# Tail of an attention and feed-forward kernel: which engine makes the remainders, and when the token blocks are renewed

## The chip, the cores and the metric

The kernel runs on one core of one Trainium2 chip. The metric is the device time of one launch, in microseconds (us). The kernel before takes 994.36 us (median of 3 runs, 994.13 to 994.58). The execution that the hardware profiler recorded took 986.7 us, of which 984.7 us are the span of instructions that the views below show.

## The reference

Attention with a forgetting factor over 4 batches, 8 heads, 576 positions and 64 dimensions is followed by two feed-forward parts on the 2304 tokens of width 512:

```python
scores = scale * np.matmul(q, k.transpose(0, 1, 3, 2)) + decay      # causal, softmax
x = np.matmul(attn, v)                                              # 2304 x 512
h = x @ w_in                                                        # 512 -> 2048
g = h * np.tanh(np.log1p(np.exp(h)))                                # mish
y = g @ w_out                                                       # 2048 -> 512
a, b = y @ w1, y @ w2                                               # 512 -> 1024 each
out = ((a * b) @ w3) @ w_out2                                       # 1024 -> 1024 -> 512
```

All of it is float32, and w3 and w_out2 are multiplied with each other ahead of use, so behind the attention there are three layers: the first one (w_in and mish), the K layer "g" (w_out), the M layer "g" (w1 and w2 and their product), and the K layer "h" (w3 times w_out2). They run for two halves of the tokens, q = 0 and q = 1.

## The kernel before, in words

**Float32 from faster products.** Every operand of a product is held as two fp32r parts: hi, a copy rounded by ScalarE, and lo, the remainder x - hi, a subtraction. TensorE makes hi*hi, hi*lo and lo*hi (`MM_PAIRS`). So each block that TensorE reads costs one ScalarE cast and one subtraction. `halves` (lines 927 to 930) writes both; the subtraction of every second block is made by VectorE and the others by GpSimd (`k % 2`).

**Seven products for eight.** Every layer multiplies 2 x 2 blocks in seven products, numbered 1 to 7, with sums and differences of blocks as operands. In a K layer (`k_layer`, n = 8 rows of blocks for g and 4 for h) the products run in `ORDER_K` = 1, 2, 6, 5, 7, 3, 4, and for each product over n tiles. One tile is twelve matmuls of 288 columns on TensorE. Its operand is made by `operand` (lines 909 to 925) from the four blocks b11, b12, b21, b22 of the source, which are renewed in place with sums (128 x 576 subtractions on VectorE): before, two of them stand behind product 2's operand (b11 and b12) and two in product 6 (its own operand raw, and b21). `k_begin` makes operands `T_AHEAD` = 4 tiles ahead; all of them live in a ring of 12 buffers (`x_tile`), two for a tile and three for a tile of product 6. Where such a layer ends, `m_operands` (line 1003 on) makes the 14 operands of the M layer from its four result blocks.

In an M layer (`m_layer`, line 1026 on) one step m is seven products of twelve matmuls; ScalarE copies some banks and VectorE adds the others (lines 1051, 1053, 1055). Products 1, 6, 7 and 4 of one m write the same bank, and between 7 and 4 only product 1 of the next m runs, so the add behind product 7 (line 1055) has that long.

**Other work in the tail.** In the first layer `s_sums` and `s_build` (lines 1091 and 1108) make weight operands for step m + 1 (sp0 and sp1, the remainder on GpSimd at line 1113), and the M layer of q = 0 builds its weights in `gate_sums` and `gate_build` (remainder on GpSimd at line 892). `x_operands` (line 1060) makes the first layer's operands while TensorE works off the last units of line 554, whose results VectorE copies out (h, line 559).

**What sets the order.** TensorE runs in written order. The other engines are placed by a scheduler that works with a simulated timeline; each of them then runs strictly in its own order, and an instruction that waits holds up all behind it on that engine. `between` makes the scheduler place instructions behind the last marked one of each engine.

Of the kernel before, what the change touches and what calls it, by code (L numbers as in the profile page):

```python
# [14 lines left out]
ALU = mybir.AluOpType  # L15
# [51 lines left out]
def f32(ap):  # L67
    return ap.bitcast(F32)
# [8 lines left out]
class Kernel:  # L77
# [807 lines left out]
    def gate_build(self, m, x, ps):  # L885

        n = len(ps)
        w = self.w_ring(f"gs{m}_{ps[0]}")
        v = w[:, :512 * n].rearrange("p (n h w) -> p n h w", n=n, h=2)
        x = x.rearrange("p (n w) -> p n w", n=n)  # L890
        self.nc.scalar.copy(v[:, :, 0], x)
        self.nc.gpsimd.tensor_tensor(v[:, :, 1], x, f32(v[:, :, 0]), ALU.subtract)
        for i, o in enumerate(ps):
            self.gate[m, o] = w[:, 512 * i:512 * i + 512]
            self.nc.sync.dma_start(self.ws[1][self.place(1, m, o)], f32(self.gate[m, o]))
# [10 lines left out]
        a, b = [t.rearrange("p (r h w) -> p r h w", r=2, h=2) for t in (src[f], src.get(f + n, src[f]))]  # L906
        return a[:, :, 0], a[:, :, 1], b[:, :, 0], b[:, :, 1]

    def operand(self, name, o, b, k):

        b11, b12, b21, b22 = b
        tt = self.nc.vector.tensor_tensor
        hi, lo = [self.x_tile(f"{name}_{x}").rearrange("p (r w) -> p r w", r=2) for x in "hl"]
        raw = {1: b11, 2: b21, 3: b22, 4: b21, 5: b11, 7: b12}.get(o)
        if o == 6:
            raw = self.x_tile(f"{name}_r", F32).rearrange("p (r w) -> p r w", r=2)
            tt(raw, b22, b11, ALU.subtract)
            self.halves(raw, hi, lo, k)
            tt(b21, b21, raw, ALU.subtract)
            return hi, lo  # L920
        self.halves(raw, hi, lo, k)
        if o == 2:
            tt(b11, b12, b11, ALU.subtract)  # L923
            tt(b12, b22, b12, ALU.subtract)
        return hi, lo

    def halves(self, raw, hi, lo, k):
        self.mark(self.nc.scalar.copy(hi, raw))  # L928
        eng = self.nc.vector if k % 2 else self.nc.gpsimd
        self.mark(eng.tensor_tensor(lo, raw, f32(hi), ALU.subtract))  # L930

    def mark(self, ins):

# [9 lines left out]
    def k_begin(self, name, n, src):  # L943

        seq = [(o, f) for o in ORDER_K for f in range(n)]
        ops = {}

        def ready(i):
            if i < len(seq) and i not in ops:
                o, f = seq[i]  # L950
                ops[i] = self.operand(f"{name}{o}_{f}", o, self.quarters(src, f, n), i)

        for i in range(T_AHEAD):
            ready(i)
        return n, seq, ops, ready
# [47 lines left out]
    def m_operands(self, q, c, T, raw, os):  # L1003

        add = self.nc.vector.tensor_tensor
        for o in os:
            for k in range(2):
                b11, b12, b21, b22 = [c[k][:, i] for i in range(4)]
                if o in (5, 6, 7, 4):
                    raw[o, k] = self.x_tile(f"r{q}_{o}_{k}", F32).rearrange("p (r w) -> p r w", r=2)  # L1010
                else:
                    raw[o, k] = {1: b11, 2: b21, 3: b22}[o]
                x = raw[o, k]
                if o == 5:
                    add(x, b12, b11, ALU.subtract)
                elif o == 6:
                    add(x, b22, raw[5, k], ALU.subtract)
                elif o == 7:
                    add(x, b22, b12, ALU.subtract)
                elif o == 4:  # L1020
                    add(x, b21, raw[6, k], ALU.subtract)
                t = self.big(0, f"T{q}_{o}_{k}", F32R) if o in (2, 4) else self.t_tile(f"T{q}_{o}_{k}")
                T[o, k] = t.rearrange("p (h r w) -> p h r w", h=2, r=2)
                self.halves(x, T[o, k][:, 0], T[o, k][:, 1], len(T))

    def m_layer(self, name, T, get, post, hook):

# [32 lines left out]
    def x_operands(self, T, os):  # L1060

        tt = self.nc.vector.tensor_tensor
        n = 0
        for o in os:
            for k in range(2):
                b11, b12, b21, b22 = [[self.xr[8 + 4 * r + c][:, TB * h:TB * h + TB] for r in range(2)]
                                      for c in (k, k + 2) for h in range(2)]
                tmp = self.tmp[:, k]
                t = self.w_ring(f"TX{o}_{k}") if o in (7, 4) else self.t_tile(f"TX{o}_{k}")
                t = T[o, k] = t.rearrange("p (h r w) -> p h r w", h=2, r=2)  # L1070
                if o == 5:
                    for r in range(2):
                        tt(tmp[:, r], b12[r], b11[r], ALU.subtract)
                elif o == 6:
                    for r in range(2):
                        tt(tmp[:, r], b22[r], tmp[:, r], ALU.subtract)
                elif o == 4:
                    for r in range(2):
                        tt(tmp[:, r], b21[r], tmp[:, r], ALU.subtract)
                elif o == 7:  # L1080
                    for r in range(2):
                        tt(b12[r], b22[r], b12[r], ALU.subtract)
                if o in (5, 6, 4):
                    self.halves(tmp, t[:, 0], t[:, 1], n)
                    n += 1
                    continue
                for r in range(2):
                    self.halves({1: b11, 2: b21, 3: b22, 7: b12}[o][r], t[:, 0, r], t[:, 1, r], n)
                    n += 1

    def s_sums(self, m):

# [15 lines left out]
    def s_build(self, m, i):  # L1108

        v = self.sp[m % 2][i].rearrange("p (n h w) -> p n h w", n=2, h=2)  # L1110
        x = self.vs[m][i].rearrange("p (n w) -> p n w", n=2)
        self.nc.scalar.copy(v[:, :, 0], x)  # L1112
        self.nc.gpsimd.tensor_tensor(v[:, :, 1], x, f32(v[:, :, 0]), ALU.subtract)  # L1113

    def first_layer(self, cover):

# [190 lines left out]
```

## Time and profile before

| | us |
|---|---|
| median of 3 runs | 994.36 |
| the profiled execution | 986.7 |
| its span | 984.7 |
| TensorE busy in the span | 891.0 |
| VectorE busy | 666.5 |
| ScalarE busy | 496.9 |
| GpSimd busy | 447.1 |

The attention part ends at about 371 us of the span. Busy time of VectorE and GpSimd in the views includes time in which an instruction has started and cannot go on, so the same instruction is long in one place and short in another; a mean over all of them hides that. "Idle before" at a row names the instruction that ended the wait.

### The profile page before, as it was taken

The page shows a single profiled execution, that of the slowest core. Times are in us where ns is not written, and L with a number is a line of the kernel's source. Part 1 is how long each engine was busy: PE and PEld are TensorE (multiplying, and loading weights), DVE is VectorE, ACT ScalarE, POOL GpSimd, SP SyncE. Part 2 cuts the span into 40 slices and gives each one's busy share as a digit, 9 for nine tenths or more (in the row PEclk, how much of TensorE's full clock was granted, in tenths as well). Part 3 has the DMA queues.
Part 4 walks back from the last instruction along what each step waited for, and adds up shares of the span by engine and source line. Part 5 has one row for each costly group of instructions (what it writes and reads, how often), then busy time and mean ns, then how long its engine had stood idle before and what let it go on. Part 6 is the DMA issues. An engine that isn't in the chain of part 4 may idle for free.

```text
span 984.7 us, 17664 instructions
## 1 busy us (share of the span) xinstructions
PE 891.0 (90%) x6336; PEld 812.4 (83%) x6336; DVE 666.5 (68%) x1148; ACT 496.9 (50%) x1091; POOL 447.1 (45%) x414
## 2 busy tenths in 40 slices
PE   0699999999999688988799998998999899999998
PEld 0467677888877468988798998998999899999998
DVE  6997796755667659677769479557549944744462
ACT  3566676755666554455533554343395344422143
POOL 4767776314745546122434577353145444400042
PEclk9899999999999799999999998999999999999999
DMA  8367679747788771333254546744976435555552
GB/s 277 118 183 225 210 233 278 205 145 223 254 269 251 224 245 55 121 129 128 76 192 153 170 160 218 298 156 162 403 250 201 152 129 171 152 164 161 167 174 73
DMA packets 129446, 185.99 MB, mean 189 GB/s; under 512 B 12160, under 2 KB 75792, under 8 KB 129360
## 3 DMA queue, kind: packets, MB, share of 16 engines
q1 hardware_dynamic: 129360, 184.88, 57.9%
q8 instruction: 50, 0.82, 0.3%
q14 instruction: 36, 0.29, 0.1%
HBM read 129.33 MB, written 55.42 MB: 188 GB/s over the span
## 4 chain that ended last, share of the span: by engine, by line
PE 60%; DVE 19%; issue 6%; DMA 6%; ACT 5%; POOL 3%; SPq 2%; DVEq 0%; ACTq 0%; POOLq 0%
PE ps_x L1040 12%; PE ps_x L968 10%; PE ps_l L554 7%; PE ps_z L1040 6%; PE ps_z L968 6%; PE ps_y L968 6%; PE ps_s L369 3%; PE ps_y L1040 3%; PE ps_s L471 2%; PE ps_l L520 2%; PE ps_t L437 2%; DVE y L923 1%; DMA ws<-pt 1%; DMA cvri<-in_w_in_dram 1%; DVE g_l L930 1%
## 5 line engine op out<-in xcount | busy, mean ns | idle before, releaser
L930 POOL TENSOR_TENSOR g_l<-y,g_h 128x576 fp32r<-128x576 f32 x48 | 79.3, 1656 | 81.4 <-ACT g_h L928 52.5
L554 PE MATMUL ps_l<-x,wi 128*128 128x288 f32 x624 | 92.8, 303 | 2.8 <-ACT h L561 2.7
L554 PEld LDWEIGHTS ps_l<-x,wi 128*128 128x128 f32 x624 | 85.6, 192 | 10.6 <-issue 5.9
L930 POOL TENSOR_TENSOR h_l<-ab,h_h 128x576 fp32r<-128x576 f32 x24 | 36.8, 1532 | 126.7 <-ACT h_h L928 117.9
L968 PE MATMUL ps_x<-g_h,ws 128*128 128x288 f32 x512 | 92.4, 299 | 1.6 <-ACT g_h L928 1.3
L928 ACT CAST g_h<-y 128x576 fp32r<-128x576 f32 x96 | 63.8, 674 | 56.5 <-PE ps_x L968 28.7
L400 ACT ACTIVATE P<-P,sum 128x256 f32<-128x256 f32 (+3 forms) x112 | 70.3, 630 | 20.1 <-DVE sum L397 14.7
L930 DVE TENSOR_TENSOR g_l<-y,g_h 128x576 fp32r<-128x576 f32 x48 | 48.8, 1020 | 45.5 <-ACT g_h L928 45.5
L968 PEld LDWEIGHTS ps_x<-g_h,ws 128*128 128x128 f32 x512 | 76.8, 191 | 2.6 <-ACT g_h L928 1.8
L369 PE MATMUL ps_s<-raw 64*128 64x128 f32 (+3 forms) x256 | 54.8, 509 | 10.2 <-DMA raw<-in_qk_dram 5.4
L968 PE MATMUL ps_x<-g_l,ws 128*128 128x288 f32 x256 | 56.4, 301 | 8.2 <-DVE g_l L930 5.3
L1040 PE MATMUL ps_x<-T,gs 128*128 128x288 f32 x384 | 56.7, 304 | 7.6 <-DVE Cg L1055 4.1
L1040 PEld LDWEIGHTS ps_x<-T,gs 128*128 128x128 f32 x384 | 54.0, 195 | 8.5 <-DVE Cg L1055 4.6
L369 PE MATMUL ps_s<-aug 64*128 64x128 f32 (+3 forms) x128 | 39.5, 600 | 20.4 <-DMA aug<-pt 20.4
L390 DVE CUSTOM_DVE_ANT_0 P<-ps_s,m 128x256 f32<-128x256 f32 (+2 forms) x96 | 49.6, 554 | 11.0 <-PE ps_s L369 10.6
L1040 PE MATMUL ps_x<-T,ws 128*128 128x288 f32 x384 | 54.2, 296 | 2.5 <-ACT x L996 1.7
L1040 PEld LDWEIGHTS ps_x<-T,ws 128*128 128x128 f32 x384 | 51.9, 189 | 3.2 <-ACT x L996 1.9
L452 DVE COPY pt<-ps_t 128x128 f32<-128x128 f32 (+1 forms) x64 | 29.5, 482 | 34.9 <-PE ps_t L437 34.7
L1113 POOL TENSOR_TENSOR sp<-sr,sp 128x512 fp32r<-128x512 f32 x14 | 23.1, 1661 | 62.7 <-ACT sp L1112 62.7
L928 ACT CAST h_h<-ab 128x576 fp32r<-128x576 f32 x48 | 31.8, 674 | 37.8 <-PE ps_x L968 22.6
L520 PE MATMUL ps_l<-wo,w3h 128*128 128x512 f32 x128 | 45.2, 422 | 5.2 <-POOL wo L113 2.9
L968 PEld LDWEIGHTS ps_x<-g_l,ws 128*128 128x128 f32 x256 | 41.4, 191 | 10.0 <-DVE g_l L930 6.8
(277 smaller groups left out, 2496.5 us busy)
## 6 DMA issues: line engine op xcount, KB each, us to landing
ws<-ws SPq DMA_DIRECT2D x112, 512.0 KB
ws<-pt SPq DMA_DIRECT2D x67, 256.0 KB
ws<-gs SPq DMA_DIRECT2D x56, 256.0 KB
h_scr<-h SPq DMA_DIRECT2D x64, 144.0 KB
y<-h_scr SPq DMA_DIRECT2D x16, 576.0 KB
cvrt<-in_w3t_dram SPq DMA_DIRECT2D x16, 512.0 KB
cvri<-in_w_in_dram SPq DMA_DIRECT2D x16, 512.0 KB
cvru<-in_w_out_dram SPq DMA_DIRECT2D x16, 512.0 KB
```

Source lines behind the costliest of these rows:

```text
L369: mm(ps[:, 512 * hh:512 * hh + n], t[r, q0:q0 + 128], t[r, 0:n], start=first, stop=not first)
L390: dve = ttr(P[hh][:, :n], ps[:, 512 * hh:512 * hh + n], self.m1[:, 512 - n:], -0.125, 3.0e38, ALU.add, ALU.min, st[hh])
L400: ins = nc.scalar.activation(t[:, :n], t[:, :n], AF.Exp, bias=b, scale=-1.0, accum_out=self.sums[:, i:i + 1])
L437: tr(self.ps_t[hh][:, o + 128 * k:o + 128 * k + 128], P[:, 128 * k:128 * k + 128], self.ident)
L452: return copy(dst[:, 0:c + 1, 128 * c:128 * c + 128], src)
L520: mm(o, w, x, start=i == 0, stop=i == 23)
L554: mm(o[:, :TB], w, x, start=i == 0, stop=i == 11)
L928: self.mark(self.nc.scalar.copy(hi, raw))
L930: self.mark(eng.tensor_tensor(lo, raw, f32(hi), ALU.subtract))
L968: mm(ps[:, r, :TB], w[:, 256 * a + 128 * e:256 * a + 128 * e + 128], ops[i][b][:, r], start=o in (1, 5, 2) and f == 0 and (a, b) == (0, 0) ...
L1040: mm(bank[:, r, :TB], w[:, i:i + 128], T[o, k][:, b, r], start=o in (1, 2, 5) and (k, a, b) == (0, 0, 0), stop=(k, a, b) == (1, 1, 0), ski ...
L1113: self.nc.gpsimd.tensor_tensor(v[:, :, 1], x, f32(v[:, :, 0]), ALU.subtract)
```

## The change

All subtractions behind the attention that make a remainder are now on VectorE: in `halves`, `gate_build` and `s_build`. The counters that chose the engine are gone. In `operand` the sums that renew the blocks are spread: one behind product 1 (b11), one behind 2 (b12), one behind 5 (b21 - b22) and one behind 7 (b21 + b11, with b11 now b12 - b11); product 6 keeps only its own operand. That is five 128 x 576 sums for a row of blocks in place of four. The renewing sums now stand inside `between`.

```diff
@@ gate_build
-        self.nc.gpsimd.tensor_tensor(v[:, :, 1], x, f32(v[:, :, 0]), ALU.subtract)
+        self.nc.vector.tensor_tensor(v[:, :, 1], x, f32(v[:, :, 0]), ALU.subtract)
@@ operand
         if o == 6:
             raw = self.x_tile(f"{name}_r", F32).rearrange("p (r w) -> p r w", r=2)
-            tt(raw, b22, b11, ALU.subtract)
-            self.halves(raw, hi, lo, k)
-            tt(b21, b21, raw, ALU.subtract)
-            return hi, lo
-        self.halves(raw, hi, lo, k)
-        if o == 2:
-            tt(b11, b12, b11, ALU.subtract)
-            tt(b12, b22, b12, ALU.subtract)
+            self.mark(tt(raw, b22, b11, ALU.subtract))
+        self.halves(raw, hi, lo)
+        with self.between():
+            if o == 1:
+                tt(b11, b12, b11, ALU.subtract)
+            elif o == 2:
+                tt(b12, b22, b12, ALU.subtract)
+            elif o == 5:
+                tt(b21, b21, b22, ALU.subtract)
+            elif o == 7:
+                tt(b21, b21, b11, ALU.add)
         return hi, lo
@@ halves
         self.mark(self.nc.scalar.copy(hi, raw))
-        eng = self.nc.vector if k % 2 else self.nc.gpsimd
-        self.mark(eng.tensor_tensor(lo, raw, f32(hi), ALU.subtract))
+        self.mark(self.nc.vector.tensor_tensor(lo, raw, f32(hi), ALU.subtract))
@@ s_build
-        self.nc.gpsimd.tensor_tensor(v[:, :, 1], x, f32(v[:, :, 0]), ALU.subtract)
+        self.nc.vector.tensor_tensor(v[:, :, 1], x, f32(v[:, :, 0]), ALU.subtract)
```

VectorE's program grows from 1143 rows to 1324: 157 remainders come from GpSimd and 24 sums are new. Three places show what this does to its order. (Line numbers from 930 on differ between the two kernels by one to three.)

The first is VectorE in a step of the first layer, from the add behind product 7 (Cx) to the next step's weights (sr are the sums for them, sp the remainders, vt a conversion of other weights). Before:

```order
L1055 TENSOR_TENSOR Cx_4307<-Cx_4307,ps_x_3932 128x576
L1103 TENSOR_TENSOR sr_2_4393<-sr_2_4393,sr_0_4391 128x256
L1105 TENSOR_TENSOR sr_3_4394<-sr_0_4391,sr_2_4393 128x256
L142 TENSOR_SCALAR vt_4452<-vt_4452 128x512
L143 SCALAR_TENSOR_TENSOR vt_4452<-tmp,vt_4452 128x512
L144 SCALAR_TENSOR_TENSOR vt_4452<-tmp,vt_4452 128x512
```

And now:

```order
L1057 TENSOR_TENSOR Cx_4307<-Cx_4307,ps_x_3932 128x576
L1102 TENSOR_TENSOR sr_2_4393<-sr_2_4393,sr_0_4391 128x256
L1104 TENSOR_TENSOR sr_3_4394<-sr_0_4391,sr_2_4393 128x256
L142 TENSOR_SCALAR vt_4452<-vt_4452 128x512
L1112 TENSOR_TENSOR sp_0_3937<-sr_2_4393,sp_0_3937 128x2x256
L143 SCALAR_TENSOR_TENSOR vt_4452<-tmp,vt_4452 128x512
L1112 TENSOR_TENSOR sp_1_3938<-sr_3_4394,sp_1_3938 128x2x256
L144 SCALAR_TENSOR_TENSOR vt_4452<-tmp,vt_4452 128x512
```

The two sp remainders stand among the conversions; before they were GpSimd's.

The second is VectorE in the K layer g of q = 0 where product 2 ends and product 6 begins (g_2_7 is tile 7 of product 2; r, h and l are raw, hi and lo; y are the blocks). Before:

```order
L930 TENSOR_TENSOR g_2_5_l<-y_13_4994,g_2_5_h 128x576
L930 TENSOR_TENSOR g_2_7_l<-y_15_5226,g_2_7_h 128x576
L917 TENSOR_TENSOR g_6_0_r<-y_8_4339,y_0_4288 128x576
L919 TENSOR_TENSOR y_8_4339<-y_8_4339,g_6_0_r 128x2x288
L917 TENSOR_TENSOR g_6_1_r<-y_9_4470,y_1_4419 128x576
L919 TENSOR_TENSOR y_9_4470<-y_9_4470,g_6_1_r 128x2x288
L930 TENSOR_TENSOR g_6_1_l<-g_6_1_r,g_6_1_h 128x576
```

And now:

```order
L932 TENSOR_TENSOR g_2_6_l<-y_14_5114,g_2_6_h 128x576
L923 TENSOR_TENSOR y_6_5069<-y_14_5114,y_6_5069 128x2x288
L932 TENSOR_TENSOR g_2_7_l<-y_15_5230,g_2_7_h 128x576
L923 TENSOR_TENSOR y_7_5203<-y_15_5230,y_7_5203 128x2x288
L917 TENSOR_TENSOR g_6_0_r<-y_8_4339,y_0_4288 128x576
L932 TENSOR_TENSOR g_6_0_l<-g_6_0_r,g_6_0_h 128x576
L917 TENSOR_TENSOR g_6_1_r<-y_9_4470,y_1_4419 128x576
L932 TENSOR_TENSOR g_6_1_l<-g_6_1_r,g_6_1_h 128x576
```

A tile of product 2 has a remainder and a sum; a tile of product 6 has its difference and right behind it the remainder, which needs ScalarE's cast of that difference.

The third is VectorE in a step of the M layer of q = 0 (Cg are the adds of the banks, vs the sums of weights, gs the remainders of weights, ab the product of the two halves). Before:

```order
L1053 TENSOR_TENSOR Cg_0_6323<-Cg_0_6323,ps_z 128x576
L1055 TENSOR_TENSOR Cg_0_6323<-Cg_0_6323,ps_x_3931 128x576
L879 TENSOR_TENSOR vs_0_6479<-vr_1_6338 128x256
L881 TENSOR_TENSOR vs_1_6480<-vr_0_6337,vr_1_6338 128x256
L1215 TENSOR_TENSOR ab_0_6457<-Cg_0_6323 128x2x288
```

And now, a step later:

```order
L1055 TENSOR_TENSOR Cg_1_6430<-Cg_1_6430,ps_z 128x576
L892 TENSOR_TENSOR gs_1_6532<-vr_0_6345,gs_1_6532 128x2x256
L1057 TENSOR_TENSOR Cg_1_6430<-Cg_1_6430,ps_x_3932 128x576
L892 TENSOR_TENSOR gs_5_6550<-vs_0_6487,gs_5_6550 128x2x256
L879 TENSOR_TENSOR vs_0_6612<-vr_1_6445 128x256
L881 TENSOR_TENSOR vs_1_6613<-vr_0_6444,vr_1_6445 128x256
L1214 TENSOR_TENSOR ab_1_6590<-Cg_1_6430 128x2x288
```

A weight remainder now stands between the add behind product 3 and the one behind product 7.

## Rows read from the trace of the kernel before

**Rows 1.** The page, busy time (share of the span) of each engine
```profile
PE 891.0 (90%) x6336; PEld 812.4 (83%) x6336; DVE 666.5 (68%) x1148; ACT 496.9 (50%) x1091; POOL 447.1 (45%) x414
```

**Rows 2.** The timeline, TensorE, first matmuls of six stages: start, duration, [idle before]
```profile
396.50 1.80 PE L1040 MATMUL ps_x<-TX,wi 128*128 128x288 f32 x12 [1.97 <-ACT TX L928]
...
503.62 0.42 PE L968 MATMUL ps_x<-g_h,ws 128*128 128x288 f32 x2
...
601.98 3.25 PE L1040 MATMUL ps_x<-T,gs 128*128 128x288 f32 x12 [3.31 <-ACT x L996]
...
700.12 0.43 PE L968 MATMUL ps_x<-h_h,ws 128*128 128x288 f32 x2
...
746.41 0.54 PE L968 MATMUL ps_x<-g_h,ws 128*128 128x288 f32 x2 [0.23 <-ACT o L996]
...
845.07 1.85 PE L1040 MATMUL ps_x<-T,ws 128*128 128x288 f32 x12 [1.67 <-ACT x L996]
```

**Rows 3.** The chain in order of time: an M layer's and a K layer's undisturbed matmuls
```profile
613.08 4.77 PE ps_x L1040 x36
...
805.00 12.80 PE ps_x L968 x96
```

**Rows 4.** The page's costliest groups: busy, mean ns, idle before
```profile
L930 POOL TENSOR_TENSOR g_l<-y,g_h 128x576 fp32r<-128x576 f32 x48 | 79.3, 1656 | 81.4 <-ACT g_h L928 52.5
...
L930 DVE TENSOR_TENSOR g_l<-y,g_h 128x576 fp32r<-128x576 f32 x48 | 48.8, 1020 | 45.5 <-ACT g_h L928 45.5
```

**Rows 5.** The timeline at 670 us, GpSimd and VectorE, the same operation
```profile
669.98 1.83 POOL L930 TENSOR_TENSOR h_l<-ab,h_h 128x576 fp32r<-128x576 f32 x1
670.44 1.99 DVE L930 TENSOR_TENSOR h_l<-ab,h_h 128x576 fp32r<-128x576 f32 x1
```

**Rows 6.** The timeline at 495 us, VectorE, while GpSimd has nothing to do
```profile
495.13 0.75 DVE L923 TENSOR_TENSOR y<-y 128x576 f32<-128x576 f32 x1
495.80 0.75 DVE L924 TENSOR_TENSOR y<-y,y 128x576 f32<-128x576 f32 x1
```

**Rows 7.** The timeline from 371 us, TensorE's last units of line 554, VectorE's copies
```profile
371.15 2.53 PE L554 MATMUL ps_z<-x,wi 128*128 128x288 f32 x12 [3.73 <-DVE xr L482]
...
386.69 1.89 PE L554 MATMUL ps_z<-x,wi 128*128 128x288 f32 x12 [1.00 <-DVE h L559]
...
392.66 1.88 PE L554 MATMUL ps_y<-x,wi 128*128 128x288 f32 x12 [0.90 <-DVE h L559]
...
395.96 0.45 DVE L559 COPY h<-ps_x 128x288 f32<-128x288 f32 x1
```

**Rows 8.** The timeline of one step of the first layer, from the casts of sp on
```profile
420.23 1.14 ACT L1112 CAST sp<-sr 128x512 fp32r<-128x512 f32 x2
420.98 3.39 POOL L1113 TENSOR_TENSOR sp<-sr,sp 128x512 fp32r<-128x512 f32 x2 [9.30 <-ACT sp L1112]
421.27 0.69 PE L1040 MATMUL ps_z<-TX,sp 128*128 128x288 f32 x4
422.71 1.33 PE L1040 MATMUL ps_z<-TX,sp 128*128 128x288 f32 x8 [0.75 <-POOL sp L1113]
```

**Rows 9.** The same wait in the first layer's last step
```profile
491.00 1.87 PE L1040 MATMUL ps_z<-TX,sp 128*128 128x288 f32 x8 [3.31 <-POOL sp L1113]
```

**Rows 10.** The timeline of TensorE in product 6 of K layer g, q = 0
```profile
544.13 0.53 PE L968 MATMUL ps_x<-g_l,ws 128*128 128x288 f32 x2 [1.45 <-DVE g_l L930]
```

**Rows 11.** The timeline: from VectorE's difference to its cast, from a cast to its remainder
```profile
521.01 0.76 DVE L917 TENSOR_TENSOR g_r<-y,y 128x576 f32<-128x576 f32 x1 [0.15 <-PE ps_z L968]
...
521.86 0.67 ACT L928 CAST g_h<-g_r 128x576 fp32r<-128x576 f32 x1 [1.79 <-DVE g_r L917]
...
678.72 0.67 ACT L928 CAST h_h<-ab 128x576 fp32r<-128x576 f32 x1 [0.44 <-DVE ab L1214]
679.49 0.76 DVE L930 TENSOR_TENSOR h_l<-ab,h_h 128x576 fp32r<-128x576 f32 x1 [0.86 <-ACT h_h L928]
```

**Rows 12.** The timeline of TensorE in the M layer of q = 0
```profile
675.14 2.69 PE L1040 MATMUL ps_x<-T,gs 128*128 128x288 f32 x12 [3.26 <-DVE Cg L1055]
```

More of the change, by code (lines that the diff above doesn't have):

```diff
@@ L907, in quarters, with operand @@
         return a[:, :, 0], a[:, :, 1], b[:, :, 0], b[:, :, 1]
-    def operand(self, name, o, b, k):
+    def operand(self, name, o, b):
         b11, b12, b21, b22 = b
@@ L916, in operand, with halves @@
             raw = self.x_tile(f"{name}_r", F32).rearrange("p (r w) -> p r w", r=2)
-            tt(raw, b22, b11, ALU.subtract)
-            self.halves(raw, hi, lo, k)
-            tt(b21, b21, raw, ALU.subtract)
-            return hi, lo
-        self.halves(raw, hi, lo, k)
-        if o == 2:
-            tt(b11, b12, b11, ALU.subtract)
-            tt(b12, b22, b12, ALU.subtract)
+            self.mark(tt(raw, b22, b11, ALU.subtract))
[9 more added lines that the diff above has]
+                tt(b21, b21, b11, ALU.add)
         return hi, lo
-    def halves(self, raw, hi, lo, k):
+    def halves(self, raw, hi, lo):
         self.mark(self.nc.scalar.copy(hi, raw))
-        eng = self.nc.vector if k % 2 else self.nc.gpsimd
-        self.mark(eng.tensor_tensor(lo, raw, f32(hi), ALU.subtract))
+        self.mark(self.nc.vector.tensor_tensor(lo, raw, f32(hi), ALU.subtract))
     def mark(self, ins):
@@ L950, in ready @@
                 o, f = seq[i]
-                ops[i] = self.operand(f"{name}{o}_{f}", o, self.quarters(src, f, n), i)
+                ops[i] = self.operand(f"{name}{o}_{f}", o, self.quarters(src, f, n))
         for i in range(T_AHEAD):
@@ L1023, in m_operands @@
                 T[o, k] = t.rearrange("p (h r w) -> p h r w", h=2, r=2)
-                self.halves(x, T[o, k][:, 0], T[o, k][:, 1], len(T))
+                self.halves(x, T[o, k][:, 0], T[o, k][:, 1])
     def m_layer(self, name, T, get, post, hook):
@@ L1062, in x_operands @@
         tt = self.nc.vector.tensor_tensor
-        n = 0
         for o in os:
@@ L1083, in x_operands @@
                 if o in (5, 6, 4):
-                    self.halves(tmp, t[:, 0], t[:, 1], n)
-                    n += 1
+                    self.halves(tmp, t[:, 0], t[:, 1])
                     continue
                 for r in range(2):
-                    self.halves({1: b11, 2: b21, 3: b22, 7: b12}[o][r], t[:, 0, r], t[:, 1, r], n)
-                    n += 1
+                    self.halves({1: b11, 2: b21, 3: b22, 7: b12}[o][r], t[:, 0, r], t[:, 1, r])
     def s_sums(self, m):
```

## The prediction, made before the changed kernel was run

> **What bounds the kernel now.** The page's busy shares come first: TensorE is busy for 90% of the span, VectorE for 68%, GpSimd for 45% [rows 1]. So time can be won only where TensorE stands still or is slowed. The change touches nothing before about 371 us, where the attention ends; I therefore read the stages behind it, by TensorE's first matmul in each [rows 2], against the pace of undisturbed matmuls: 36 in 4.77 us in an M layer, 96 in 12.80 us in a K layer [rows 3], both 0.133 us each. A product of twelve takes 1.59 to 1.60 us.
>
> Eight steps of seven products are 56 x 12 x 0.1325 = 89.0 us, K layer g has 56 tiles, 89.6 us, K layer h 28, 44.8 us. The stages took [rows 2]: first layer 503.62 - 396.50 = 107.1 (18.1 over); K g, q = 0, 98.4 (8.8 over); M, q = 0, 98.1 (9.1 over); K h, q = 0, 46.3 (1.5 over); K g, q = 1, 98.7 (9.1 over). That is 46.6 us of standstill and slow matmuls.
>
> What TensorE waits for in them is mostly a remainder or something queued behind one. GpSimd's remainder has a mean of 1656 ns, VectorE's of the same shape 1020 ns [rows 4]. The second number is a mix. While GpSimd worked on one, VectorE's took 1.99 us [rows 5]; where GpSimd had nothing to do, VectorE's 128 x 576 operations took 0.75 us and started 0.67 us after one another [rows 6]. So GpSimd's remainders cost twice: they are slow, and they hold VectorE up. The wait at 675.14 us names VectorE, but the add there came behind that operation of 1.99 us [rows 5, 12].
>
> **The change part by part.** 157 remainders leave GpSimd and 24 sums are added on VectorE. At 0.67 us a 128 x 576 operation, a tile of products 1, 2, 5 and 7 costs VectorE two operations, 1.34 us, against 1.60 us of TensorE: it keeps up. Over a K layer g it is (56 remainders + 40 sums) x 0.67 = 64.3 us in 89.6. The 0.67 holds only if GpSimd is what made VectorE slow; the ends are 0.67 and 1.02 [rows 4, 6], and I take 0.67, the row in which GpSimd is idle, since it will always be.
>
> The Trainium skill has a rule against this: by "VectorE: DVE Perf Modes", section "The DRAIN you can't avoid", the next VectorE operation does not start until the pipe is empty (with an exception for operations that are not held), so each would cost its whole 0.75 us. The starts 0.67 us apart speak against it here; what it would do is a rival below.
>
> *The last units before the first layer.* TensorE has twelve units of 1.6 us, 19.2 us, from 371.15 us, the first at a slower pace; it waited 1.00 and 0.90 for VectorE's copies of results, and the first layer began at 396.50 after 1.97 us, just behind such a copy (395.96 + 0.45) [rows 2, 7]. The row names a cast, but the copy is what ended then. These copies stand in one queue with operations stretched by GpSimd. VectorE now has 13 more remainders there, yet none is stretched. Gain at most 1.00 + 0.90 + 1.97 = 3.9, at least 1; I take 3.5, near the upper end, because all three waits have one cause.
>
> *First layer.* In five of the steps TensorE waits 0.75 us for GpSimd's remainder [rows 8]; one of the five is shown. ScalarE's two casts start at 420.23 and take 1.14 together, so the first is there at about 420.85; VectorE's remainder, of 512 columns, takes at most 0.75 and ends by 421.6. TensorE needs it after four matmuls, 421.27 + 4 x 0.133 = 421.8. The wait goes, and with its restart I count 0.8 x 5 = 4.0. What is late next is the add behind product 7, which the change leaves in its place. In the last step the wait is 3.31 [rows 9], and there the remainder stands behind eight operands of the next layer in VectorE's order: mostly this stays, I count 1.5. Sum 5.5; ends 2 and 9.
>
> *K layer g, q = 0.* The two sums per tile behind product 2 are spread, but product 6 is a chain: difference, cast, remainder, next difference. From the difference's start to the cast's is 521.86 - 521.01 = 0.85; from a cast's start to its remainder's 679.49 - 678.72 = 0.77 [rows 11]; then 0.67 to the next: 2.29 us per tile against 1.60. Eight tiles fall behind by 8 x 0.69 = 5.5 us. The ring of 12 buffers gives a lead of four tiles of three; one of them is just being made free, so the operand can be begun 3 x 1.60 = 4.8 us before use: a margin of 4.8 - 2.29 + 0.27 (two matmuls of hi go first) = 2.8. So about 2.7 us of wait remain; I count 2.5, as the adds of product 2's banks fall into the waits for casts. The waits there now, 1.45 the longest shown [rows 10], are of like size in sum. The end of the layer is different: 3.31 us of wait before the M layer's first product, which then took 3.25 for 1.6 us of work [rows 2]. VectorE there has 23 operations of 128 x 576 behind the add of product 3 (3 tiles' remainders, 8 differences and 12 remainders for the M layer), 23 x 0.67 = 15.4 us, and nine narrower ones, some 4: 19.5 us. Product 4 (12.8 us) and three products of the M layer (4.8) pass before the last operand of product 2 is wanted: 17.6. So 1.5 to 2 us are late instead of 6; they fall into the next stage. Of 8.8 over, 2.5 stay: gain 6.3, ends 2 and 8.8.
>
> *M layer, q = 0.* Four weight remainders per step go to VectorE: 13 operations, at most 0.67 each, 8.7 of 11.1 us. The wait of 3.26 and the slow product behind it (2.69 for 1.6) [rows 12] have GpSimd's weight remainders as cause; VectorE, alone, gets through the same queue in time. I leave 1.5 at the head and 1.3 that I do not itemise: gain 9.1 - 2.8 = 6.3, ends 1 and 9.1. Each weight remainder between two adds adds a wait for ScalarE's cast, and the add behind it is what product 4 waits for; the room is one product, 1.6 us. In the trace ScalarE's casts come well ahead, but that cover is why the lower end is so low.
>
> *K layer g, q = 1, and its end.* The same without weights: 9.1 over, 2.5 stay: gain 6.6, ends 2 and 9.1. The other stages have next to nothing to win, and product 6 of K layer h is only four tiles, inside its lead. GpSimd's removal and the dropped counters cost nothing: nothing else behind the attention is on GpSimd's queue.
>
> Sum: 3.5 + 5.5 + 6.3 + 6.3 + 6.6 = 28.2 us. Against the profiled execution, 986.7 - 28.2 = 958.5. That execution is 7.7 below the median of the runs, 994.36; I carry the difference over: 994.36 - 28.2 = 966.
>
> **The rivals.**
> *VectorE's chains pace the K layers.* If most remainders wait for their cast as in product 6, VectorE's own order becomes the bound. For: 2.29 against 1.60 us, and the buffers that hold the lead are shared with the operands of the M layer. Against: in the other products the casts need nothing of VectorE's. Each tile of products 1, 2, 5 and 7 that fell to 2.29 would cost 0.69; with half of the 64 in two K layers g, 22 us, less what the lead takes up, some 14 remain: 980.
> *The M layer's queue ends slower than before.* A weight remainder waits for a cast that stands behind a copy from TensorE's bank; the add behind it is late, product 4 stands still. The price is that of [rows 12]: 3.26 + (2.69 - 1.6) = 4.4 us a step. It decides if seven or more of the steps of the first layer and the M layer have it: at nine, 39.6 us against a gain of 28.2, about 1006. Against: VectorE is busy for 8.7 of 11.1 us.
> *GpSimd is not the cause of VectorE's long operations.* Then 96 operations x 1.02 = 98 us in a K layer g, 8 us over its 89.6, in addition to what is over now; the same in the M layers' operands: 994 + 2 x 8 + 4 = 1014. Against: 0.75 and 1.99 for the same shape [rows 5, 6].
> *The whole pipe time per operation.* 0.08 us more per operation. Tiles at 1.50 still keep up; the two chains of product 6 lose 8 x 0.08 each, the two queues at the layers' ends 23 x 0.08 = 1.8 each: about 5 us, 971.
> *More than I count.* If the first layer's last step and product 6 are fully hidden, and the add behind product 7 also comes earlier: 10 us more, 956.
>
> **How the numbers follow.** Chances: forecast (gain of 22 to 35 us) 0.66; chains pace the K layers 0.13; more than I count 0.09; whole pipe time 0.04; no net change because gains and new waits cancel 0.02; the M layer's queue 0.04; GpSimd not the cause 0.02. The ends of the terms added up are 8 and 40 us; not all are at one end at once, so 956 to 980 holds the forecast, the cheap pipe case and most of both neighbours, somewhat over 8 in 10. Within 0.2% (2 us, about what a measurement of this kernel can tell from no change) has 0.02, slower 0.06, faster 0.92.
>
> **What would show it.** In the changed profile VectorE's 128 x 576 operations behind 371 us have a mean near 0.75 us. GpSimd is empty there. TensorE's stage starts lie closer: K g and its end at about 92 us, M of q = 0 at about 92, the first layer at 101 to 102. The wait for sp in the first layer is gone in the middle steps and stays near 2 to 3 us in the last. Product 6 shows the longest waits in K g, for a remainder by VectorE. The forecast is wrong if VectorE's mean stays near 1 us, if waits for casts stand before most remainders of products 1, 2, 5 and 7, or if the adds of the M layer come late behind a weight remainder.

## The result, and the profile after

The changed kernel takes 961.51 us (median of 4 runs, 958.19 to 962.9) against 994.47 us for the kernel before beside it: ratio 0.966, 95% interval 0.9622 to 0.9697. It is faster by 33.0 us; 28.4 were predicted. Its profiled execution took 958.19 us with a span of 956.4 (before 986.7 and 984.7).

The page's busy times answer to [rows 1], its groups to [rows 4]:

```profile
PE 883.2 (92%) x6336; PEld 807.2 (84%) x6336; DVE 687.5 (72%) x1329; ACT 496.3 (52%) x1091; POOL 203.4 (21%) x257
...
L932 DVE TENSOR_TENSOR g_l<-y,g_h 128x576 fp32r<-128x576 f32 x96 | 72.1, 754 | 19.2 <-ACT g_h L931 18.3
...
L932 DVE TENSOR_TENSOR h_l<-ab,h_h 128x576 fp32r<-128x576 f32 x48 | 35.9, 755 | 13.6 <-ACT h_h L931 13.4
```

VectorE took over 157 remainders and 24 sums and is busy for only 21.0 us more, because its operations became shorter: the mean of the same remainder fell from 1020 to 754 ns. GpSimd's 244 us are gone.

The timeline of TensorE, the stage starts that answer to [rows 2] and the first of the last units that answers to [rows 7] (start, duration, [idle before]):

```profile
377.26 2.68 PE L554 MATMUL ps_z<-x,wi 128*128 128x288 f32 x12 [3.58 <-DVE xr L482]
...
398.64 1.82 PE L1042 MATMUL ps_x<-TX,wi 128*128 128x288 f32 x12 [0.56 <-issue]
...
499.20 0.42 PE L970 MATMUL ps_x<-g_h,ws 128*128 128x288 f32 x2
...
589.56 1.75 PE L1042 MATMUL ps_x<-T,gs 128*128 128x288 f32 x12
...
680.77 0.43 PE L970 MATMUL ps_x<-h_h,ws 128*128 128x288 f32 x2
...
727.07 0.53 PE L970 MATMUL ps_x<-g_h,ws 128*128 128x288 f32 x2 [0.24 <-ACT o L998]
...
817.09 1.75 PE L1042 MATMUL ps_x<-T,ws 128*128 128x288 f32 x12
```

| stage, us | before | after | gain | predicted |
|---|---|---|---|---|
| last units before the first layer | 25.35 | 21.38 | 4.0 | 3.5 |
| first layer | 107.1 | 100.6 | 6.6 | 5.5 |
| K g, q = 0 | 98.4 | 90.4 | 8.0 | 6.3 |
| M, q = 0 | 98.1 | 91.2 | 6.9 | 6.3 |
| K h, q = 0 | 46.3 | 46.3 | 0 | 0 |
| K g, q = 1 | 98.7 | 90.0 | 8.6 | 6.6 |
| the rest | 139.6 | 139.3 | 0.3 | 0 |

The stages sum to 34.4 us. The profiled executions differ by only 28.5, since the attention ahead, which is the same in both, ended 6.1 us later in this one (377.26 against 371.15). It ends between 374.9 and 381.9 us in the profiles of the runs below, 377.8 in the mean with this one, so some 6.6 of the 7.7 us by which the profiled execution of before lay under its median lay there.

### The profile page after: what moved, and what is told of

Same layout as the page of the kernel before. It is cut to its first block, busy times and chain, and to the rows that moved or that the text cites. A ratio compares the mean times of both kernels' runs of the same rounds, so it can differ in the third digit from the quotient of the medians.

```text
span 956.4 us, 17581 instructions
## 1 busy us (share of the span) xinstructions
PE 883.2 (92%) x6336; PEld 807.2 (84%) x6336; DVE 687.5 (72%) x1329; ACT 496.3 (52%) x1091; POOL 203.4 (21%) x257
## 4 chain that ended last, share of the span: by engine, by line
PE 72%; DVE 9%; DMA 7%; ACT 4%; issue 4%; POOL 2%; SPq 2%; ACTq 0%; DVEq 0%; POOLq 0%
PE ps_x L970 14%; PE ps_x L1042 14%; PE ps_z L1042 7%; PE ps_y L970 6%; PE ps_z L970 6%; PE ps_l L554 6%; PE ps_s L369 4%; PE ps_y L1042 3%; PE ps_l L520 3%; PE ps_t L437 2%; PE ps_s L471 2%; PE ps_s L373 2%; DMA cvri<-in_w_in_dram 1%; DMA cvru<-in_w_out_dram 1%; DMA ws<-pt 1%
## 5 line engine op out<-in xcount | busy, mean ns | idle before, releaser
L932 DVE TENSOR_TENSOR g_l<-y,g_h 128x576 fp32r<-128x576 f32 x96 | 72.1, 754 | 19.2 <-ACT g_h L931 18.3
L400 ACT ACTIVATE P<-P,sum 128x256 f32<-128x256 f32 (+3 forms) x112 | 70.4, 631 | 21.6 <-DVE sum L397 16.1
L1042 PE MATMUL ps_x<-T,gs 128*128 128x288 f32 x384 | 54.1, 296 | 1.7 <-ACT Cg L1047 0.9
L1042 PEld LDWEIGHTS ps_x<-T,gs 128*128 128x128 f32 x384 | 51.9, 188 | 2.2 <-ACT Cg L1047 1.1
L931 ACT CAST h_h<-ab 128x576 fp32r<-128x576 f32 x48 | 31.6, 671 | 39.1 <-PE ps_x L970 21.8
L970 PE MATMUL ps_x<-h_h,ws 128*128 128x288 f32 x256 | 46.4, 297 | 0.1
L932 DVE TENSOR_TENSOR h_l<-ab,h_h 128x576 fp32r<-128x576 f32 x48 | 35.9, 755 | 13.6 <-ACT h_h L931 13.4
L471 PE MATMUL ps_s<-pt,va 128*64 128x320 f32 (+3 forms) x384 | 45.0, 383 | 0.0
L437 PE MATMUL ps_t<-ident,P 128*128 128x128 f32 x288 | 40.6, 276 | 2.8 <-DVE pt L452 1.9
```

The costliest lines, as they stand in the source:

```text
L400: ins = nc.scalar.activation(t[:, :n], t[:, :n], AF.Exp, bias=b, scale=-1.0, accum_out=self.sums[:, i:i + 1])
L437: tr(self.ps_t[hh][:, o + 128 * k:o + 128 * k + 128], P[:, 128 * k:128 * k + 128], self.ident)
L471: mm(ps[64 * hh:64 * hh + 64, 256 + q:256 + q + w], lhs, rhs, start=i == 0, stop=i == len(plan) - 1)
L932: self.mark(self.nc.vector.tensor_tensor(lo, raw, f32(hi), ALU.subtract))
L970: mm(ps[:, r, :TB], w[:, 256 * a + 128 * e:256 * a + 128 * e + 128], ops[i][b][:, r], start=o in (1, 5, 2) and f == 0 and (a, b) == (0, 0) ...
L1042: mm(bank[:, r, :TB], w[:, i:i + 128], T[o, k][:, b, r], start=o in (1, 2, 5) and (k, a, b) == (0, 0, 0), stop=(k, a, b) == (1, 1, 0), ski ...
```

## The experiments

Stage lengths below are differences between TensorE's first matmuls. For K g, q = 1, the very first is taken: the row at 746.41 in [rows 2], and at 727.07 above, stands 1.2 us behind it. Differences of about 1 us between single cells are not explained here: with the same matmuls TensorE is busy for 562.5 us behind the attention in the profile of the changed kernel and for 566.1 in that of run 1.

| us | time | last units | first layer | K g q0 | M q0 | K g q1 |
|---|---|---|---|---|---|---|
| before | 994.5 | 25.4 | 107.1 | 98.4 | 98.1 | 99.9 |
| after | 961.5 | 21.4 | 100.6 | 90.4 | 91.2 | 91.2 |
| 1 sums put back | 962.3 | 21.4 | 101.9 | 91.5 | 92.0 | 92.3 |
| 2 engines put back | 982.3 | 25.4 | 107.5 | 95.8 | 93.5 | 93.6 |
| 3 weights on GpSimd | 973.1 | 21.6 | 108.7 | 90.7 | 98.0 | 91.2 |
| 4 blocks on GpSimd | 971.5 | 25.0 | 104.1 | 95.8 | 92.5 | 93.6 |
| 5 added subtraction | 986.6 | 21.8 | 101.4 | 101.6 | 94.7 | 101.4 |
| 6 added zeros | 962.7 | 21.4 | 102.3 | 90.8 | 91.6 | 90.8 |
| 7 added copy (one run) | 964.8 | 21.4 | 101.0 | 94.2 | 91.9 | 94.5 |
| 8 third buffer | 959.9 | 22.0 | 100.8 | 90.9 | 91.2 | 90.9 |
| 9 weight sums earlier | 953.3 | 21.4 | 94.2 | 90.9 | 91.2 | 91.2 |
| 10 and operands later | 952.2 | 21.4 | 93.2 | 91.7 | 91.2 | 91.2 |

**1. The sums alone put back.**

```diff
-        with self.between():
-            if o == 1:
-                tt(b11, b12, b11, ALU.subtract)
...
+        if o == 2:
+            tt(b11, b12, b11, ALU.subtract)
+            tt(b12, b22, b12, ALU.subtract)
+        elif o == 6:
+            tt(b21, b21, raw, ALU.subtract)
```

> All remainders stay on VectorE; the sums that renew the token blocks go back to where they stood before (two per tile at product 2, one per tile at product 6). Theory A (GpSimd held VectorE up, the place of the sums is secondary): a tile of product 2 costs VectorE 3 x 0.67 = 2.0 us against 1.60 of TensorE, 8 tiles fall behind by 3.3 us, within the lead of 4.8; in product 6 the third operation can go into the wait for the cast. Loss 0 to 3 us in each K layer g, time 962 to 968, I say 965. Theory B (the gain comes from the spread sums): most of the K layers' 16.6 us come back, about 978.

962.29 us, ratio to before 0.9661 (0.9618 to 0.9704): nothing that can be told from the changed kernel. The timeline of its VectorE and ScalarE in product 6 shows why product 6 does not mind:

```profile
522.61 0.75 DVE L917 TENSOR_TENSOR g_r<-y,y 128x576 f32<-128x576 f32 x1
523.40 0.76 DVE L923 TENSOR_TENSOR y<-y,g_r 128x576 f32<-128x576 f32 x1
523.45 0.68 ACT L927 CAST g_h<-g_r 128x576 fp32r<-128x576 f32 x1 [1.55 <-DVE g_r L917]
524.16 0.76 DVE L928 TENSOR_TENSOR g_l<-g_r,g_h 128x576 fp32r<-128x576 f32 x1
```

The sum (L923) runs while the cast is made, and the tile takes 2.23 us with it as without it (522.61 to the next difference at 524.84). The stages in the table sum to 4.3 us more than the changed kernel's, but TensorE's waits in them, from the start of the first layer on, only to 0.8 more (12.8 against 12.0 us); the rest is the 3.5 us for which TensorE is busy longer with the same matmuls. Theory B falls.

**2. The engines alone put back**, sums spread: `halves` alternates again, `gate_build` and `s_build` use GpSimd.

```diff
-        self.mark(self.nc.vector.tensor_tensor(lo, raw, f32(hi), ALU.subtract))
+        eng = self.nc.vector if k % 2 else self.nc.gpsimd
+        self.mark(eng.tensor_tensor(lo, raw, f32(hi), ALU.subtract))
```

> The sums stay spread; every remainder goes back to the engine it had before (alternating in the K layers, all of the weights on GpSimd). Theory A: the gain is lost, VectorE's 128x576 remainders are near 1.0 us in the mean and K layer g takes 95 to 98 us; time 985 to 994, I say 990. Theory B: VectorE has fewer remainders and spread sums, time 961 to 968. If theory A holds, the time minus the one before is also what spreading alone is worth.

982.31 us (0.9805 to 0.9904 of before). The engines matter, and VectorE's remainders are back at 0.96 us in K g and 1.02 in K h in the mean, but 985 to 994 was a miss: spreading the sums is worth some 13 us while GpSimd works on remainders (K g q1 99.9 to 93.6, M q0 98.1 to 93.5), and nothing that the times can tell once it does not (0.8 us between the medians of run 1 and the changed kernel). The two parts are not additive; the change of engine alone brings the whole 33 us. Why spreading helps beside GpSimd was not tried.

**3 and 4. The two halves of that.** 3: only the weights' remainders on GpSimd; 4: only the blocks', every second one (run 2 with the two lines below on VectorE).

```diff
 # 3, gate_build and s_build
-        self.nc.vector.tensor_tensor(v[:, :, 1], x, f32(v[:, :, 0]), ALU.subtract)
+        self.nc.gpsimd.tensor_tensor(v[:, :, 1], x, f32(v[:, :, 0]), ALU.subtract)
```

> Only the weights' remainders (14 in the first layer, 24 in the M layer of q = 0) go back to GpSimd, the token blocks' stay on VectorE. Theory A: the first layer has its wait of 0.75 us for a remainder back in five steps (about +4 us), K g with q = 0 and the M layer behind it see VectorE operations of up to 2 us and gain 3 to 6 us of length; K g with q = 1 and its M layer stay at 90.0 and 91 us. Time 969 to 973. Rival: GpSimd's slowness is hidden by the lead of the weights, and only the token blocks' remainders counted: 961 to 964.

> The complement of the run with the weights on GpSimd: every second remainder of the token blocks and of the M and first layers' operands on GpSimd, the weights' remainders on VectorE, sums spread. If the two halves add up (all on GpSimd cost 982.3 - 961.5 = 20.8 us, the weights' alone 11.6), 9 us: time 970 to 972. If they interfere only with each other, 962 to 966.

973.07 and 971.51 us: 11.6 and 10.0 us over the changed kernel, 21.6 together against 20.8 for both, so they add up. Each is lost where it works: the weights in the first layer (+8.1, where about 4 was expected) and M q0 (+6.8; K g q0, which was to lose with it, did not), the blocks in the last units, the first layer and K g. The timeline of kernel 3 at the head of M q0, GpSimd and VectorE:

```profile
595.39 10.93 POOL L892 TENSOR_TENSOR gs<-vs,gs 128x512 fp32r<-128x512 f32 x1 [4.89 <-ACT gs L891]
596.73 0.74 DVE L932 TENSOR_TENSOR T<-r,T 128x576 fp32r<-128x576 f32 x1
...
602.75 1.42 DVE L932 TENSOR_TENSOR T<-r,T 128x576 fp32r<-128x576 f32 x2
604.08 0.41 DVE L879 TENSOR_TENSOR vs<-vr 128x256 f32<-128x256 f32 x1
604.42 0.41 DVE L881 TENSOR_TENSOR vs<-vr,vr 128x256 f32<-128x256 f32 x1
604.75 0.41 DVE L880 TENSOR_TENSOR vs<-vs,vr 128x256 f32<-128x256 f32 x1
605.20 1.40 DVE L882 TENSOR_TENSOR vs<-vr,vs 128x256 f32<-128x256 f32 x1
```

The hold goes both ways. GpSimd's remainder stands for 10.93 us (others of its kind in this kernel 1.28) as long as VectorE's operations follow each other without a gap, and they are not slowed. The operations of 0.41 us start 0.34 and 0.33 us apart; the last one starts 0.45 behind its neighbour, 0.1 late, and takes 1.40, and GpSimd's ends at 606.32. So GpSimd seems to have got in through that gap, and the 1.66 us of [rows 4] were in part its own waiting.

**5. A GpSimd operation that nobody waits for.**

```diff
         self.halves(raw, hi, lo)
+        if k % 2 == 0:
+            x = f32(hi)[:, :, :252]
+            self.nc.gpsimd.tensor_tensor(self.ghost, x, x, ALU.subtract)
```

> The changed kernel with one added GpSimd operation at every second tile of the K layers (subtract, 128x504 f32, reads the rounded half, writes a scratch tile that nobody reads): nothing waits for its result. Theory A (contention): it takes GpSimd about 1.45 us, VectorE's operation beside it goes from 0.75 to 1.7 to 2.0 us; 28 x 1.1 = 31 us more on VectorE in a K layer g (64 of 89.6 used before), so K g is 3 to 7 us longer and the M layer's head is late: time 970 to 980, I say 974. Rival C (GpSimd was merely slow, so what waited for it was late): VectorE stays at 0.75, stages as in the changed kernel, 961 to 963.

986.55 us (0.9874 to 0.9934 of before): 25 us lost, more than the 8 to 18 expected, and K g is longer than it was before the change. The timeline at the head of K g, GpSimd and VectorE:

```profile
504.18 0.76 DVE L937 TENSOR_TENSOR g_l<-y,g_h 128x576 fp32r<-128x576 f32 x1 [4.25 <-ACT g_h L936]
504.23 1.59 POOL L923 TENSOR_TENSOR ghost<-g_h 128x504 f32<-128x504 f32 x1 [8.73 <-ACT g_h L936]
504.97 1.47 DVE L926 TENSOR_TENSOR y<-y 128x576 f32<-128x576 f32 x1
...
507.43 1.36 POOL L923 TENSOR_TENSOR ghost<-g_h 128x504 f32<-128x504 f32 x1 [1.61 <-ACT g_h L936]
507.82 1.58 DVE L937 TENSOR_TENSOR g_l<-y,g_h 128x576 fp32r<-128x576 f32 x1
```

One VectorE operation per added one takes 1.47 to 1.6 instead of 0.75; the one at 504.97 reads and writes only y, not the tile that GpSimd reads. Inside K g, q = 0, 25 operations are held, for 20 us in all, and where a difference of product 6 is held, the whole chain behind it is later: TensorE waited 8.7 us for g_l and 5.0 for g_h in all, 0.5 and 1.0 in the changed kernel. Rival C falls for the K layers: no result of GpSimd's was late, for nothing used one. The buffer of the rounded half, which is not free before GpSimd has read it, is hardly the reason: the added operations start right behind their casts and are through with it in 1.0 to 1.7 us.

**6 and 7. What about the GpSimd operation holds VectorE?** In place of the subtraction, 6 has three fills with zeros, 7 a copy.

```diff
-            self.nc.gpsimd.tensor_tensor(self.ghost, x, x, ALU.subtract)
+            self.nc.scalar.copy(self.ghost[:, 0, 0:1], f32(hi)[:, 0, 0:1])
+            for _ in range(3):
+                self.nc.gpsimd.memset(self.ghost, 0.0)
 # 7
+            self.nc.gpsimd.tensor_copy(self.ghost, x)
```

> As the kernel with the added GpSimd operation at every second tile of the K layers, but GpSimd fills the scratch tile with zeros three times in a row there (it writes and reads nothing in SBUF), behind a one-column copy by ScalarE of the rounded half. Theory A1 (VectorE is held while GpSimd reads SBUF and VectorE has two SBUF inputs): VectorE's 128x576 operations stay at 0.75 us, K g at 90 to 92 us, time 961 to 966 (84 one-column copies on ScalarE lie in its idle time). Theory A2 (any GpSimd operation holds VectorE): VectorE's mean is 0.9 us or more, K g 95 to 102 us, time 975 to 990.

> As the kernel with the added GpSimd subtraction at every second tile of the K layers, with a copy (one SBUF input) in its place. Theory A1 (a GpSimd operation that reads SBUF holds a VectorE operation with two SBUF inputs, however many inputs it has itself): VectorE's operation beside it takes 0.75 us plus nearly the copy's time, VectorE's mean for 128x576 remainders is over 0.82 us. Rival (the hold needs GpSimd's second input): all stay at 0.75 us, as beside the fill with zeros.

The timeline of kernel 6, then of kernel 7:

```profile
805.35 1.67 POOL L924 MEMSET ghost<- 128x504 f32 x3 [1.53 <-ACT ghost L922]
806.64 0.76 DVE L938 TENSOR_TENSOR g_l<-y,g_h 128x576 fp32r<-128x576 f32 x1 [0.84 <-ACT g_h L937]
```

```profile
780.76 0.67 POOL L923 COPY ghost<-g_h 128x504 f32<-128x504 f32 x1 [2.42 <-ACT g_h L936]
780.88 1.16 DVE L937 TENSOR_TENSOR g_l<-y,g_h 128x576 fp32r<-128x576 f32 x1
781.96 0.75 DVE L932 TENSOR_TENSOR y<-y,y 128x576 f32<-128x576 f32 x1
```

Beside the fills (252 of them, 131 us of GpSimd) VectorE's remainders keep a mean of 751 ns and the time is 962.69 us. Beside the copy they take up to 1.16, 809 ns in the mean (over 820 was expected), and each K g is 3.3 to 3.8 us longer. So it is GpSimd's reading that holds VectorE, with one input as with two; the copy holds for less time (0.41 us against 0.83), as it is shorter (0.67 us in the row above, the subtraction 1.03 where it was least).

The other side is in kernel 2: the add behind product 3, one of whose inputs is a TensorE bank, beside a weight remainder on GpSimd:

```profile
665.79 1.28 POOL L892 TENSOR_TENSOR gs<-vs,gs 128x512 fp32r<-128x512 f32 x1
666.55 0.75 DVE L1056 TENSOR_TENSOR Cg<-Cg,ps_z 128x576 f32<-128x576 f32 x1 [0.85 <-PE ps_z L1043]
```

It is not held. Of the 72 adds of that kind in the first and the M layers, 16 run beside a GpSimd operation there, and none of these takes over 0.76 us, while the renewing sums, both of whose inputs lie in SBUF (where the tiles are), have means of up to 1365 ns.

The Trainium skill says this in "SBUF — State Buffer", section "Who interferes with whom": a VectorE instruction with two SBUF inputs contends with a GpSimd instruction that reads SBUF, not with one that only writes it; the port pair that the two share is an exclusive lock, and the order of issue decides who blocks. The rows of kernels 2, 6 and 7 agree on which operations contend (0.75 us with a bank among the inputs and beside the fills, 1.16 beside the copy). On the order, kernel 3 goes further: by its rows VectorE's operations from 596.73 on began behind GpSimd's and went through ahead of it all the same.

**8. A smaller lead for product 6.**

```diff
+        if o == 2:
+            pad = self.x_tile(f"{name}_p", F32)
+            self.nc.scalar.copy(pad[:, 0:1], f32(hi)[:, 0, 0:1])
```

> The changed kernel, but each tile of product 2 takes a third buffer of the ring of 12 (it is given one column and not used), so that the chain of product 6 begins with a lead of four tiles, as the prediction counted, and not with the lead that tiles of two buffers give (its first difference stood at 517.16, its first matmul near 524.8, 7.6 us). If the lead is what made the wait of product 6 only 0.9 and 0.6 us where 2.5 was predicted, it is now 2 to 3 us in each K g and both K g are 1 to 2.5 us longer; time 962 to 966. If the chain itself is shorter than counted, the waits stay below 1 us: 960 to 962.

959.93 us, just below both ranges; the waits of product 6 in K g q0 are 0.31 and 0.26. But the edit did not do its work: the first difference still stands at 521.70, 7.3 us ahead of product 6's first matmul at 529.04. The lead was not cut, perhaps because the added buffer, which nobody reads, came free at once; no row shows that. Inconclusive.

**9 and 10. What is left in the first layer.**

```diff
-                    if o == 2:
+                    if o == 6:
                         self.s_sums(m + 1)
 # 10, in addition
+                with self.between():
                     self.begun = self.k_begin("g0_", 8, self.y)
```

> The changed kernel with one line moved: in the first layer the six sums of the next step's weights are issued behind product 6 instead of behind product 2, where VectorE idles for some 3 us a step. Theory: what is left over in the first layer (100.6 us against 89.0) is the add behind product 7, which stands behind the sums on VectorE's queue (0.55 us of wait and some 0.25 of restart in seven steps, 5.6 us), and the last step, where the sums come so late that cast and remainder stand behind the next layer's operands (3.3 us). Both go: first layer 92 to 95 us, time 952 to 956, I say 954. Rival: the add is late for another reason, or the casts of the weights now hold up VectorE in front of that same add: 960 to 963.

> As the kernel with the sums of the next step's weights behind product 6, and in addition the first eight operands of K layer g are bound behind the add of the last step but one, where they now stand in front of it (a wait of 1.95 us at 479.83 with matmuls at a slower pace behind it, and 0.85 at 491.99). Theory (the add is late only because of these operands): the wait of 1.95 goes, first layer 94.15 to 91 to 92.5 us, time 950 to 952.5, I say 951. Rival: the operands are then late for K layer g itself, which waits as long: 953 to 955.

953.28 us (0.9546 to 0.9604 of before, below the interval of the changed kernel): of the seven waits for the add five are gone, those for sp in the last step are gone too, and the first layer takes 94.15. With the operands placed later 952.17 us (0.9538 to 0.9613): not to be told from it, with the first layer at 93.2 (91 to 92.5 expected). The timelines of TensorE in the first layer, all its waits behind the start, of 9 and of 10:

```profile
479.83 2.72 PE L1042 MATMUL ps_x<-TX,wi 128*128 128x288 f32 x12 [1.95 <-DVE Cx L1057]
491.99 1.85 PE L1042 MATMUL ps_x<-TX,wi 128*128 128x288 f32 x12 [0.85 <-DVE Cx L1057]
```

```profile
487.18 2.48 PE L1042 MATMUL ps_x<-TX,wi 128*128 128x288 f32 x12 [3.06 <-DVE Cx L1057]
```

In run 10 the same operands now stand ahead of the next step's add, and the wait moved there: 1.95 + 0.85 became 3.06.

## Why the prediction was right

**The cause.** The main step was that GpSimd costs twice, by being slow and by holding VectorE up, and that 0.67 us between starts holds once it is idle. The timeline of the changed kernel's VectorE in K g:

```profile
536.00 0.75 DVE L932 TENSOR_TENSOR g_l<-y,g_h 128x576 fp32r<-128x576 f32 x1
536.67 0.75 DVE L925 TENSOR_TENSOR y<-y 128x576 f32<-128x576 f32 x1
537.34 0.75 DVE L932 TENSOR_TENSOR g_l<-y,g_h 128x576 fp32r<-128x576 f32 x1
```

The starts are 0.67 us apart, as in [rows 6], and the mean duration is 754 ns, so the rival of the whole pipe time falls. The rule that the prediction drew from the Trainium skill ("VectorE: DVE Perf Modes", section "The DRAIN you can't avoid") would have put the starts 0.75 apart, if these operations were held; they agree with the exception that the section makes for a next operation that is not held, which starts earlier. The rival by which GpSimd is not the cause falls by runs 5 to 7. How the 33 us divide between GpSimd's slowness and its hold was not measured; run 5 shows that the hold alone, with no result waited for, can cost 25. By run 1 the spreading of the sums is worth nothing that the times can tell; the prediction named it only as a part of K g and gave it no term of its own.

**Last units, 3.5 predicted, 4.0 measured.** The waits of 1.00 and 0.90 for the copies [rows 7] are gone, and the start of the first layer waits 0.56 instead of 1.97: 3.3 us, the rest being the slower start behind each wait. By run 4 it is the blocks' remainders on GpSimd that cost them (25.0).

**First layer, 5.5 predicted, 6.6 measured.** The timeline of TensorE, one step and the last one, which answer to [rows 8] and [rows 9]:

```profile
421.72 1.85 PE L1042 MATMUL ps_x<-TX,wi 128*128 128x288 f32 x12 [0.55 <-DVE Cx L1057]
423.40 1.75 PE L1042 MATMUL ps_z<-TX,sp 128*128 128x288 f32 x12
...
485.33 0.79 PE L1042 MATMUL ps_z<-TX,sp 128*128 128x288 f32 x4 [1.72 <-ACT sp L1111]
...
487.70 2.29 PE L1042 MATMUL ps_z<-TX,sp 128*128 128x288 f32 x8 [1.59 <-DVE sp L1112]
...
497.52 1.85 PE L1042 MATMUL ps_x<-TX,wi 128*128 128x288 f32 x12 [0.85 <-DVE Cx L1057]
```

The timeline of TensorE in the kernel before, the add's last two waits:

```profile
485.16 1.86 PE L1040 MATMUL ps_x<-TX,wi 128*128 128x288 f32 x12 [1.25 <-DVE Cx L1055]
...
501.93 1.86 PE L1040 MATMUL ps_x<-TX,wi 128*128 128x288 f32 x12 [1.72 <-DVE Cx L1055]
```

The wait for sp is gone in the middle steps, and the add behind product 7 is what is late there, 0.55 us as before. The split was off: a step became 1.0 us shorter (12.97 to 11.96), not 0.8, while the last step's wait for sp gave nothing of the 1.5 counted: 1.72 + 1.59 = 3.31, as before. There the cast is late as well, because the weights' sums stand behind operands of K g; run 9 moved the sums and the wait went. That the term still came near is luck: the add's last two waits, from which nothing was counted, fell from 1.25 and 1.72 to 0.55 and 0.85, 1.6 us, in place of the 1.5.

**K g, 6.3 and 6.6 predicted, 8.0 and 8.6 measured: the mis-sized term.** The prediction left 2.5 us of wait in product 6. The timeline of the first difference and of the waits, answering to [rows 10] and [rows 11]:

```profile
517.16 0.75 DVE L917 TENSOR_TENSOR g_r<-y,y 128x576 f32<-128x576 f32 x1
518.02 0.67 ACT L931 CAST g_h<-g_r 128x576 fp32r<-128x576 f32 x1 [2.37 <-DVE g_r L917]
518.72 0.76 DVE L932 TENSOR_TENSOR g_l<-g_r,g_h 128x576 fp32r<-128x576 f32 x1 [0.82 <-ACT g_h L931]
519.40 0.76 DVE L917 TENSOR_TENSOR g_r<-y,y 128x576 f32<-128x576 f32 x1
...
524.39 0.42 PE L970 MATMUL ps_x<-g_h,ws 128*128 128x288 f32 x2
...
535.35 0.53 PE L970 MATMUL ps_x<-g_h,ws 128*128 128x288 f32 x2 [0.64 <-ACT g_h L931]
...
536.14 0.54 PE L970 MATMUL ps_x<-g_l,ws 128*128 128x288 f32 x2 [0.26 <-DVE g_l L932]
```

The chain is as counted: 2.24 us a tile (2.29), only the two tiles with the adds of product 2's banks among them took 2.7. The wait is 0.90 us in all, 0.62 with q = 1, and the longer part is for the cast, not the remainder. What was mis-sized is the lead: 4.8 us were counted, from four tiles of three buffers, but the first difference stood 7.2 us before product 6's first matmul (524.39 - 517.16). By these rows 2.4 us less of lead would have left 0.90 + 2.4 = 3.3 us of wait, an estimate, where 2.5 were counted. The trace of the kernel before had it already. Its timeline of TensorE, the first matmul of product 6:

```profile
528.82 0.42 PE L968 MATMUL ps_x<-g_h,ws 128*128 128x288 f32 x2
```

The first difference there stands at 521.01 [rows 11], 7.8 us ahead. Why the lead is that long is not shown: the tiles ahead of product 6 have two buffers and not three, which would fit, but run 8, which was to test it, did not cut the lead.

The 1.5 to 2 us that were to be late at the layer's end are not seen there; the M layer starts at 589.56 without a wait.

**M, q = 0, 6.3 predicted, 6.9 measured.** The timeline of TensorE, its two waits there:

```profile
593.78 1.85 PE L1042 MATMUL ps_x<-T,gs 128*128 128x288 f32 x12 [0.87 <-ACT Cg L1047]
...
679.09 1.85 PE L1042 MATMUL ps_x<-T,gs 128*128 128x288 f32 x12 [0.85 <-DVE Cg L1057]
```

The wait of 3.26 [rows 12] is gone, and 0.87 and 0.85 are left where 1.5 and 1.3 were counted. The second has nothing to do with the weights: the M layer of q = 1, which makes no weight remainder, has the same 0.85 in its last step. TensorE waits for no add behind a weight remainder in the steps between, so the rival of the M layer's queue did not come. With the weights' remainders back on GpSimd (run 3) the wait is back and the layer is 6.8 us longer; VectorE's operations ahead of that add take up to 1.85 us. The timelines of TensorE, M layer of q = 1 in the changed kernel, then M layer of q = 0 in kernel 3:

```profile
905.48 1.85 PE L1042 MATMUL ps_x<-T,ws 128*128 128x288 f32 x12 [0.85 <-DVE Cg L1057]
```

```profile
670.72 3.15 PE L1042 MATMUL ps_x<-T,gs 128*128 128x288 f32 x12 [4.35 <-DVE Cg L1057]
```

**The sum.** 28.2 predicted, 34.4 in the stages: 3.7 of the 6.2 more lie in the two K g. All five terms came out above what was predicted. The prediction took the row at 746.41 for the first matmul of K g, q = 1; that stands at 745.22, so 0.3 us and not 1.5 were over in K h, and 10.3 and not 9.1 in K g. Both kernels have these 1.2 us, so no gain changes. Carrying the profiled execution's distance from the median over was right, as most of that distance lay in the attention.

## What to carry to other kernels

A second engine that takes half of an operation is no help if its reads hold the first one up: look for one form of instruction with two durations (here 0.75 and 1.99 us), and see what runs beside the long ones. Before moving work between two engines, price the hold by adding an operation that nobody waits for. Where the trace of the kernel before has the chain, read its lead off the rows, from the chain's first instruction to the first one that needs it, and do not count it in buffers: here 7.8 us stood there and 4.8 were counted.

## What the runs showed of the hardware that was not expected

- GpSimd was kept out for nearly all of 10.93 us by VectorE operations without a gap, and seems to have got in through a gap of 0.1 us (run 3).
- GpSimd's writing alone costs VectorE nothing: 252 fills of 520 ns, VectorE at 751 ns (run 6); nor does its reading, if one of VectorE's inputs comes from a TensorE bank: at most 0.76 us in 16 such adds (run 2).
- An added GpSimd subtraction, 1.5 us in the mean, held one VectorE operation for 0.83 us, and with one at every second tile a layer of 90 us became 10 to 11 us longer (run 5).
